# Second mixture of experts: the second product with the activations stationary and w2 streaming, 16 of 144 tokens on four column tiles

## Chip, cores, metric

One core of a Trainium2 chip runs the whole program. The metric is the device time of one execution in microseconds (us). PE is TensorE (matmul), PEld its loading of stationary operands, DVE VectorE, ACT ScalarE, POOL GpSimd, SP SyncE.

## What is computed

```python
attn_out = _attn_ref(q, k, v)                       # 2 x 8 heads x 576 x 64, with rotary positions
x = attn_out.transpose(0, 2, 1, 3).reshape(1152, 512)
x = _moe_ref(x, w_gate, w1, w2)                     # every expert for every token, weighted
return _moe2_ref(x, w_gate, w1, w2)                 # one expert for each token

def _moe2_ref(x, w_gate, w1, w2):
    N, D = x.shape; E = w_gate.shape[1]; cap = N // E      # 1152, 512, 8, 144
    logits = x @ w_gate
    ...                                             # greedy: best pairs first, at most cap tokens an expert
    for e in range(E):
        mask = assigned == e
        out[mask] = np.maximum(x[mask] @ w1[e], 0.0) @ w2[e]     # w1[e] 512x1024, w2[e] 1024x512
```

All data are float32. The change touches only the loop at the end, the second mixture: eight experts of exactly 144 tokens each.

## The kernel before

The attention takes the first 150 us or so, the first mixture lasts until about 945 us, and the second mixture (`moe2`, from L167) ends the program. Its tokens lie in a DRAM buffer `ysc`, row by row.

The assignment runs in phases (`phase(p)`). A phase finds, on DVE and PE, one expert that is full and its 144 tokens: `bcast` (L206) transposes the tokens' best logits, `compare` (L225) and `count` (L235, L241) count how many are better, `assign`, `total` and `close` find the full expert, `left` (L278) adds the phase's tokens to `ac` on POOL, `select` (L284) takes this expert's tokens, `place` (L300) and `spread` (L308) give each a slot and a one-hot row `hot`, and `index` (L316) multiplies `hot` with the token numbers: two groups of nine matmuls, 72 slots each. `address` makes row numbers of them, `gather` (L331) fetches the rows from `ysc` with two indirect DMAs on POOL into `xa` and `xb`, 72 tokens each, and `weights` (L344) issues eight DMAs of 512 KB on SP for w1 and w2 of this expert.

An expert (`expert(p)`, L404) then does four things on PE, all in plain float32:
- `tin` (L407): in two halves, transposes `xa` and `xb` (L413, L414), so that features lie on partitions: `xg`, 128 x 4 x 144. ACT copies them out of PSUM (L415).
- `h_mm` (L417, L422): 8 x 4 calls, stationary a 128x128 block of w1, moving 144 tokens; ACT applies the Relu into `h`, 128 x 8 x 144 (L425).
- `y_mm` (L427, L432): 4 x 8 calls, stationary a 128x128 block of w2, moving the 144 tokens of `h`; the result has features on partitions, and ACT copies it into `y` (L435).
- `tout` (L437, L441): two times four transposes bring tokens back onto partitions; ACT copies (L442), and `scatter` (L444) writes 72 rows a time to `out` with indirect DMAs on POOL (L447).

What stands where is set by a small planner (`Plan`, L121). Each step is added with the steps that it waits for and with its estimated durations per engine, as ("PE", 0.246, 0.0); the products (`main=True`) form a line whose order is fixed, and all other steps are emitted when the estimate says that they can start, before a product if they are earlier. The whole step is emitted at once, its ACT part with its PE part, so this order is also that of ACT's, DVE's and POOL's queues. A mark ("tn", p) keeps the input transposes of an expert from being placed earlier than `LEAD` products before its first one. PSUM tiles come from a ring of four banks (`ybank`).

Of the kernel before, what the change touches and what calls it, by code (L numbers as in the profile page):

```python
# [21 lines left out]
F32 = mybir.dt.float32  # L22
# [10 lines left out]
CAP = N // E  # L33
HC = CAP // 2
NT = N // 128
# [61 lines left out]

def moe2_consts(nc, one, rt):
# [12 lines left out]
    nc.gpsimd.tensor_copy(c["meta"].rearrange("p t k -> p (t k)"), rc[:, 288:324])  # L111
    for n, shape, dt, val in (("ones_b", [128, 128], BF, 1.0), ("pen", [128, E], F32, 0.0), ("u", [128, NT], F32, 1.0),
                              ("rem", [128, E], F32, float(CAP)), ("ac", [128, NT, E], F32, 0.0)):
        c[n] = one.tile(shape, dt, name=n)
        nc.gpsimd.memset(c[n], val)
    c["spacer"] = one.tile([1, 1], F32, name="spacer")
    c["tick"] = one.tile([1, 1], I32, name="tick")
    return c
# [44 lines left out]

CFG = dict(CG=3, NCMP=6, HA=20, LEAD=8, FILL=24)


def moe2(tc, nc, ctx, ps, m1, w1b, w2b, ident, lg, ysc, out):  # L167
    BIG = 3.0e38
    FAR = 1.0e6
    if True:  # L170
# [19 lines left out]
        def phase(p):  # L190
# [125 lines left out]
            def index():  # L316
                pi = ps.tile([128, 512], F32, name="PV", bufs=1)[0:HC, 0:8]
                for h in range(2):
                    for t in range(NT):
                        nc.tensor.matmul(pi[:, 4 * h:4 * h + 4], d["hot"][:, t, h * HC:(h + 1) * HC], meta[:, t],  # L320
                                         start=(t == 0), stop=(t == NT - 1))
                d["pi"] = pi

            def address():
                f = two.tile([HC, 8], F32, name="idf")
                V.tensor_copy(f, d["pi"])
                ix = two.tile([HC, 4], I32, name="ix", bufs=8)
                V.scalar_tensor_tensor(ix, f[:, 0:8:2], 128.0, f[:, 1:8:2], op0=OP.mult, op1=OP.add)
                d["ix"] = ix

            def gather():  # L331
                if "p" not in X:
                    m1.mst.close()
                    X["p"] = ctx.enter_context(tc.tile_pool(name="m2x", bufs=2))
                xa = X["p"].tile([HC, D], F32, name="xa")
                xb = X["p"].tile([HC, D], F32, name="xb")
                for h, x in enumerate((xa, xb)):
                    G.indirect_dma_start(out=x, out_offset=None, in_=ysc,
                                         in_offset=bass.IndirectOffsetOnAxis(ap=d["ix"][:, 2 * h:2 * h + 1], axis=0))
                d["xa"], d["xb"] = xa, xb  # L340
                if p == 0:
                    G.memset(tick, 0)

            def weights(lo, hi):  # L344
# [59 lines left out]
        def expert(p):  # L404
            d = S_[p]

            def tin(h):  # L407
# [3 lines left out]
                for k in range(2):  # L411
                    o = slice((2 * h + k) * 128, (2 * h + k + 1) * 128)
                    nc.tensor.transpose(pt[:, k, 0:HC], d["xa"][:, o], ident[0:HC, 0:HC])  # L413
                    nc.tensor.transpose(pt[:, k, HC:CAP], d["xb"][:, o], ident[0:HC, 0:HC])  # L414
                nc.scalar.activation(Z["xg", p][:, 2 * h:2 * h + 2], pt, AF.Copy)  # L415

            def h_mm(f, kt):  # L417
                if f == 0 and kt == 0:
                    Z["h", p] = X["p"].tile([128, FB, CAP], F32, name="h")
                if f % 2 == 0 and kt == 0:  # L420
# [3 lines left out]
                if f % 2 and kt == KT - 1:  # L424
                    nc.scalar.activation(Z["h", p][:, f - 1:f + 1], Z["ph"], AF.Relu)  # L425

            def y_mm(b, f):  # L427
                if b == 0 and f == 0:
                    Z["y", p] = X["p"].tile([128, KT, CAP], F32, name="y")
                if b % 2 == 0 and f == 0:  # L430
                    Z["py"] = m1.ybank()[:, 0:2 * CAP].rearrange("p (k c) -> p k c", k=2)
                nc.tensor.matmul(Z["py"][:, b % 2], d["wb"][f // 4][:, f % 4, b * 128:(b + 1) * 128],  # L432
                                 Z["h", p][:, f], start=(f == 0), stop=(f == FB - 1))
                if b % 2 and f == FB - 1:
                    nc.scalar.activation(Z["y", p][:, b - 1:b + 1], Z["py"], AF.Copy)  # L435

            def tout(h):  # L437
                o = Z["o", p, h] = X["p"].tile([HC, D], F32, name="o" + "ab"[h])
                pt = m1.ybank()
                for k in range(KT):  # L440
                    nc.tensor.transpose(pt[0:HC, k * 128:(k + 1) * 128], Z["y", p][:, k, h * HC:(h + 1) * HC], ident)  # L441
                nc.scalar.activation(o, pt[0:HC], AF.Copy)  # L442

            def scatter():  # L444
                for h in range(2):
                    G.memset(spacer, 0.0)
                    s = G.indirect_dma_start(  # L447
                        out=out, out_offset=bass.IndirectOffsetOnAxis(ap=d["ix"][:, 2 * h + 1:2 * h + 2], axis=0),
                        in_=Z["o", p, h], in_offset=None)
                    for q in scat:  # L450
                        tc.declare_no_dep(s.ins, q.ins, reason="each token has one expert")
                    scat.append(s)

# [10 lines left out]
            for b in range(4):  # L464
                for f in range(FB):
                    end = f == FB - 1 and b % 2
                    seg = [("PE", 0.246, 0.2), ("ACT", 0.29, 0.15)] if end else [("PE", 0.246, 0.0)]
                    op("yend" if end and b == 3 else ("y", b, f), ["whi", f"h{f | 1}"], seg, y_mm, b, f, main=True)
            for h in range(2):
                op(f"to{h}", ["yend"] + (["to0"] if h else []), [("PE", 0.5, 0.2), ("ACT", 0.6, 0.1)], tout, h)  # L470
            op("sc", ["to1"], [("POOL", 2.1, 0.0)], scatter)

# [21 lines left out]
        for p in range(1, E):  # L494
            plan.mark(("tn", p), nf + 2 * FB * KT * p - CFG["LEAD"])
        plan.run()
# [6 lines left out]
class Moe1:  # L503
# [37 lines left out]
    def open2(self):  # L541
# [4 lines left out]
        c2 = st.enter_context(tc.tile_pool(name="m2c", bufs=1))  # L546
        self.c2 = moe2_consts(nc, c2, self.rt)
        self.mst = ExitStack()
# [995 lines left out]
```

## Time and profile before

| | |
|---|---|
| time, median of 3 runs | 1132.48 us (1130.39 to 1133.1) |
| the profiled execution's own time | 1128.46 us |
| its span from first to last instruction | 1126.5 us |
| mean granted clock of PE | 0.998 |
| PE busy | 1101.4 us, 98% |
| DVE, ACT, POOL busy | 761.1, 367.6, 451.2 us |

The page gives the busy time of each engine, then the span in 40 slices of 28 us, then the chain of work that ended last. The second mixture's products fill the last six slices. Idle time of an engine costs only where another, which sets the end, waits for it. Matmuls overlap in the engine, so the duration of one is longer than its distance to the next; distances are read from the timeline.

### The profile page before, as it was taken

How to read it: one execution, taken by the hardware profiler on the slowest of the kernel's cores; microseconds unless marked ns; L12 is line 12 of the kernel's file. 1: busy time of each engine (PE TensorE's matmuls, PEld its weight loads, DVE VectorE, ACT ScalarE, POOL GpSimd, SP SyncE). 2: the span in 40 equal slices, each digit the busy share in tenths (PEclk: the TensorE clock that was granted, in tenths of full speed). 3: DMA queues.
4: the chain of work that ended last, by engine and by line, in shares of the span. 5: the costliest groups of instructions: out<-in, count | busy, mean ns of one | idle time of the engine just before them, and what ended most of it. 6: DMA issues, size and time to landing. Idle time of an engine off the chain costs nothing. (4 is left out here: it accounts for less than half of the span.)

```text
span 1126.5 us, 20911 instructions
## 1 busy us (share of the span) xinstructions
PE 1101.4 (98%) x8171; PEld 959.3 (85%) x8171; DVE 761.1 (68%) x1713; ACT 367.6 (33%) x846; POOL 451.2 (40%) x446
## 2 busy tenths in 40 slices
PE   6999999999999999999999999999999999999997
PEld 3666678998888889898888898998989876999997
DVE  5777733574677778777777776666679887988100
ACT  5777742143223232232232322333231111222222
POOL 6878452065434345444354443444210001554211
PEclk9999999999999999999999999999999999999999
DMA  5332322002222323332223321121140004978820
GB/s 130 79 74 50 98 81 76 1 1 71 83 87 88 94 76 105 112 94 83 87 87 126 97 70 62 39 75 38 38 150 29 1 29 141 351 242 289 278 76 22
DMA packets 105314, 107.22 MB, mean 95 GB/s; under 512 B 35456, under 2 KB 68608, under 8 KB 105088
## 3 DMA queue, kind: packets, MB, share of 16 engines
q1 hardware_dynamic: 102528, 100.66, 28.5%
q0 software_dynamic: 2048, 4.72, 1.3%
q8 instruction: 64, 1.05, 0.4%
q10 hardware_dynamic: 640, 0.51, 0.2%
q14 instruction: 34, 0.28, 0.1%
HBM read 98.85 MB, written 4.72 MB: 92 GB/s over the span
## 5 line engine op out<-in xcount | busy, mean ns | idle before, releaser
L929 DVE SCALAR_TENSOR_TENSOR acc<-Y,pw,acc 128x512 f32<-128x512 f32 x216 | 158.2, 742 | 1.5 <-PE Y L927 0.4
L865 PE MATMUL T<-xH,wa 128*128 128x256 f32 (+1 forms) x576 | 137.5, 294 | 0.2 <-ACT v L885 0.2
L865 PEld LDWEIGHTS T<-big,wb 128*128 128x128 f32 x864 | 125.7, 188 | 10.5 <-DVE v L878 1.4
L878 DVE TENSOR_TENSOR v<-T,v 128x256 f32<-128x256 f32 (+1 forms) x240 | 108.3, 451 | 38.6 <-PE T L865 35.8
L865 PE MATMUL T<-big,wb 128*128 128x256 f32 (+1 forms) x864 | 132.7, 296 | 0.0
L865 PEld LDWEIGHTS T<-xH,wa 128*128 128x128 f32 x576 | 100.0, 188 | 7.8 <-ACT v L885 1.9
L682 PE MATMUL T<-xH,wa 128*128 128x384 f32 x336 | 92.9, 337 | 0.0
L774 POOL TENSOR_TENSOR wa<-wraw,wa 128x512 fp32r<-128x512 f32 (+1 forms) x48 | 48.9, 1019 | 103.6 <-ACT wa L773 103.6
L865 PE MATMUL T<-xL,wa 128*128 128x256 f32 (+1 forms) x288 | 84.5, 293 | 0.0
L872 DVE SCALAR_TENSOR_TENSOR hlB<-v,hhB 128x320 fp32r<-128x320 f32 x72 | 57.0, 791 | 38.7 <-ACT hhB L871 38.7
L871 ACT ACTIVATE hhB<-v 128x320 fp32r<-128x320 f32 x72 | 34.0, 472 | 136.2 <-DVE v L878 136.2
L871 ACT ACTIVATE hhA<-v 128x256 fp32r<-128x256 f32 x72 | 30.1, 418 | 146.8 <-DVE v L878 146.8
L927 PE MATMUL Y<-wb,hhB 128*128 128x512 f32 x240 | 75.3, 396 | 0.0
L927 PE MATMUL Y<-wa,hhB 128*128 128x512 f32 x240 | 75.3, 395 | 0.0
L872 DVE SCALAR_TENSOR_TENSOR hlA<-v,hhA 128x256 fp32r<-128x256 f32 x72 | 50.5, 702 | 35.3 <-ACT hhA L871 35.3
L1000 DVE SCALAR_TENSOR_TENSOR fr<-fr,fc 128x512 f32<-128x512 f32 x64 | 52.5, 820 | 31.0 <-DMA fr<-in_moe_w 31.0
L793 POOL TENSOR_TENSOR wb<-wraw,wb 128x512 fp32r<-128x512 f32 x24 | 30.6, 1298 | 102.2 <-ACT wb L792 102.2
L793 POOL TENSOR_TENSOR wa<-wraw,wa 128x512 fp32r<-128x512 f32 x24 | 30.6, 1295 | 100.0 <-ACT wa L792 100.0
L701 PE MATMUL Y<-wb,hh 128*128 128x512 f32 x216 | 68.3, 397 | 0.0
L682 PEld LDWEIGHTS T<-xH,wa 128*128 128x128 f32 x336 | 61.3, 188 | 2.9 <-issue 0.9
L1352 DVE TENSOR_REDUCE negmax<-S 128x1 f32<-128x576 f32 x72 | 53.9, 749 | 14.4 <-PE S L1343 13.4
L927 PE MATMUL Y<-wa,hhA 128*128 128x512 f32 x192 | 60.0, 393 | 0.0
(323 smaller groups left out, 2668.3 us busy)
## 6 DMA issues: line engine op xcount, KB each, us to landing
wraw<-in_moe_w SPq DMA_DIRECT2D x52, 512.0 KB, 5.2
fr<-in_moe_w SPq DMA_DIRECT2D x64, 256.0 KB, 4.4
wraw<-in_moe_w SPq DMA_DIRECT2D x48, 256.0 KB, 3.2
big<-in_moe_w SPq DMA_DIRECT2D x20, 512.0 KB, 7.4
wa<-in_moe_w SPq DMA_DIRECT2D x18, 512.0 KB, 5.5
wb<-in_moe_w SPq DMA_DIRECT2D x14, 512.0 KB, 7.6
fc<-in_moe_w_gate SPq DMA_DIRECT2D x9, 256.0 KB, 3.5
ysc<-acc SPq DMA_DIRECT2D x9, 256.0 KB, 2.1
```

The lines of the kernel that those rows point to most:

```text
L682: nc.tensor.matmul(p[:, :CH], w[:, wi, kt, (fb % 2) * 128:(fb % 2) * 128 + 128], x[:, kt, o], start=(n == 0), stop=(n == 11))
L701: nc.tensor.matmul(self.Y[c][t], a[:, o], w[:, wi, fb % 2], start=(fb == 0 and n == 0), stop=(fb == FB - 1 and n == 2))
L774: G.tensor_tensor(l, src, h.bitcast(F32), op=OP.subtract)
L793: G.tensor_tensor(d["W"][:, 1, h], r[:, 2 + h], d["W"][:, 0, h].bitcast(F32), op=OP.subtract)
L865: nc.tensor.matmul(bank[:, 0:n], d[t][:, ww, b, r * 128:(r + 1) * 128], x(xw, r), start=(first and i == 0), stop=(i == 5), skip_group_chec ...
L871: A.activation(HH[:, f, o], src, AF.Relu)
L872: V.scalar_tensor_tensor(HL[:, f, o], src, 0.0, HH[:, f, o].bitcast(F32), op0=OP.max, op1=OP.subtract)
L878: V.tensor_tensor(o, bank[:, 0:n], x, op=OP.add)
L927: nc.tensor.matmul(y, h[:, f, o], w[:, ww, f], start=(f == 0 and z == 0), stop=(f == 1 and z == 2))
L929: V.scalar_tensor_tensor(self.acc[:, t], y, self.pw[:, t, e:e + 1], self.acc[:, t], op0=OP.mult, op1=OP.add)
L1000: nc.vector.scalar_tensor_tensor(r, r, 1.0, self.fc, op0=OP.mult, op1=OP.mult, accum_out=self.wf[:, f, e:e + 1])
L1352: V.tensor_reduce(m[0:n], SS[P, i][0:n, :, :288], axis=AX.XY, op=OP.max, negate=True)
```

## The change

The second product is turned round. For 128 of an expert's 144 tokens `h` is now the stationary operand (128 features x 128 tokens) and a row block of w2 moves, 512 columns: 8 calls in place of 32, and the result has tokens on partitions, so the output transposes go. The other 16 tokens (`RM`) are done by `y_rm`: eight calls with 32 stationary columns (16 tokens and 16 zero columns, for which `h` is padded to 160), dealt out over four column tiles of the array by their PSUM partitions 0, 32, 64 and 96, two calls each. ACT copies the four partial sums into `r`, and `add` sums them with a matmul by a constant 0/1 matrix `pick` (128x16), built at the start on POOL. The gathers and scatters are of 128 and 16 rows, so the input transposes are of 128 and of 16 tokens. `LEAD` is 4, and the planner gets new estimates: 0.46 us for a call of `y_mm`, 1.0 for `y_rm`, 0.5 for `add`.

```diff
-HC = CAP // 2
+RM = 16
+MN = CAP - RM
...
+    c["pick"] = one.tile([128, RM], F32, name="pick")
+    nc.gpsimd.tensor_tensor(c["pick"], ident[:, 0:RM], ident[:, 32:32 + RM], op=OP.add)
+    for i in (64, 96):
+        nc.gpsimd.tensor_tensor(c["pick"], c["pick"], ident[:, i:i + RM], op=OP.add)
...
-CFG = dict(CG=3, NCMP=6, HA=20, LEAD=8, FILL=24)
+CFG = dict(CG=3, NCMP=6, HA=20, LEAD=4, FILL=24)
...
-                        nc.tensor.matmul(pi[:, 4 * h:4 * h + 4], d["hot"][:, t, h * HC:(h + 1) * HC], meta[:, t],
+                        nc.tensor.matmul(pi[:, 4 * h:4 * h + 4], d["hot"][:, t, (RM, 0)[h]:(CAP, MN)[h]], meta[:, t],
...
+                    X["h"] = [X["p"].tile([128, FB, CAP + RM], F32, name=f"h{i}", bufs=1) for i in range(2)]
+                xa = X["p"].tile([MN, D], F32, name="xa")
+                xb = X["p"].tile([RM, D], F32, name="xb")
...
                 if p == 0:
                     G.memset(tick, 0)
+                    for t in X["h"]:
+                        G.memset(t[:, :, CAP:], 0.0)
...
-                    nc.tensor.transpose(pt[:, k, 0:HC], d["xa"][:, o], ident[0:HC, 0:HC])
-                    nc.tensor.transpose(pt[:, k, HC:CAP], d["xb"][:, o], ident[0:HC, 0:HC])
+                    nc.tensor.transpose(pt[:, k, 0:MN], d["xa"][:, o], ident)
+                    nc.tensor.transpose(pt[:, k, MN:CAP], d["xb"][:, o], ident[0:RM, 0:RM])
...
+            def y_mm(f):
+                if f == 0:
+                    Z["py"] = m1.ybank()
+                nc.tensor.matmul(Z["py"], Z["h", p][:, f, 0:MN], d["wb"][f // 4][:, f % 4], start=(f == 0),
+                                 stop=(f == FB - 1))
+
+            def y_rm():
+                Z["pr"] = m1.ybank()
+                for f in range(FB):
+                    o = f % 4 * 32
+                    nc.tensor.matmul(Z["pr"][o:o + 32], Z["h", p][:, f, MN:MN + 32], d["wb"][f // 4][:, f % 4],
+                                     start=(f < 4), stop=(f >= 4))
+                Z["r", p] = X["p"].tile([128, D], F32, name="r")
+                nc.scalar.activation(Z["r", p], Z["pr"], AF.Copy)
+
+            def add():
+                nc.tensor.matmul(Z["pr"][0:RM], c2["pick"], Z["r", p], start=True, stop=True)
+                o = Z["o", p, 1] = X["p"].tile([RM, D], F32, name="ob")
+                nc.scalar.activation(o, Z["pr"][0:RM], AF.Copy)
+
+            def tout():
+                o = Z["o", p, 0] = X["p"].tile([MN, D], F32, name="oa")
+                nc.scalar.activation(o, Z["py"], AF.Copy)
...
+            for f in range(FB + 1):
+                at = 6 if p == E - 1 else FB
+                if f == at:
+                    op("rm", ["whi", f"h{FB - 1}"], [("PE", 1.0, 0.2), ("ACT", 0.6, 0.1)], y_rm, main=True)
+                if f < FB:
+                    end = f == FB - 1
+                    op("yend" if end else ("y", f), ["whi", f"h{f | 1}"], [("PE", 0.46, 0.2 if end else 0.0)], y_mm, f,
+                       main=True)
+            op("to", ["yend"], [("ACT", 0.6, 0.1)], tout)
+            op("add", ["rm"], [("PE", 0.5, 0.2), ("ACT", 0.6, 0.1)], add)
             for h in range(2):
-                op(f"to{h}", ["yend"] + (["to0"] if h else []), [("PE", 0.5, 0.2), ("ACT", 0.6, 0.1)], tout, h)
-            op("sc", ["to1"], [("POOL", 2.1, 0.0)], scatter)
+                op(f"sc{h}", [("to", "add")[h]], [("POOL", 1.1, 0.0)], scatter, h)
...
-            plan.mark(("tn", p), nf + 2 * FB * KT * p - CFG["LEAD"])
+            plan.mark(("tn", p), nf + (FB * KT + FB + 1) * p - CFG["LEAD"])
```

In the changed file L422 and L423 are the input transposes, L431 is the first product, L439 the second (128 tokens), L446 the 16 tokens, L452 the sum over the tiles, L458 the copy of the 128 rows, L462 the scatter.

Three places show how the planner's order changes. The first is PE at the border from expert 6 to expert 7. Before:

```order
L432 MATMUL Y<-h,wa 128x144
L413 MATMUL Y<-ident,xa 128x72
L414 MATMUL Y<-ident,xb 128x72
L413 MATMUL Y<-ident,xa 128x72
L414 MATMUL Y<-ident,xb 128x72
L432 MATMUL Y<-h,big_11964 128x144 x4
L422 MATMUL Y<-xg,big_12106 128x144 x2
L422 MATMUL Y<-xg,wraw 128x144
L441 MATMUL Y<-ident,y 72x128 x4
```

The same border with the change:

```order
L439 MATMUL Y<-big_11966,h_10114 128x512 x2
L422 MATMUL Y<-ident,xa 128x128
L423 MATMUL Y<-ident,xb 128x16
L422 MATMUL Y<-ident,xa 128x128
L423 MATMUL Y<-ident,xb 128x16
L446 MATMUL Y<-wa,h_10114 32x512 x4
L446 MATMUL Y<-big_11966,h_10114 32x512 x4
L452 MATMUL Y<-r,pick 16x512
L431 MATMUL Y<-xg,big_12101 128x144 x2
```

The output transposes between the next expert's first products are gone; the 16 tokens' calls stand between the input transposes and the next expert, and here the sum L452 follows them at once (one border earlier four calls of L431 stand between).

The second place is the end of ACT's queue, the copies of the last expert. Before:

```order
L425 ACTIVATE h<-Y 128x288 x4
L435 ACTIVATE y<-Y 128x288 x2
L442 ACTIVATE oa<-Y 72x512
L442 ACTIVATE ob<-Y 72x512
L1540 UNCONDITIONAL_BRANCH
```

With the change:

```order
L434 ACTIVATE h_10115<-Y 128x2x144 x4
L449 ACTIVATE r<-Y 128x512
L454 ACTIVATE ob<-Y 16x512
L458 ACTIVATE oa<-Y 128x512
L1559 UNCONDITIONAL_BRANCH
```

The copy of the 16 rows now stands ahead of that of the 128 rows, and POOL's last two scatters stand in the same order.

The third place is POOL's queue in the middle of the assignment, around the second scatter of a row pair. Before:

```order
L338 DMA xa<-ysc,ix 72x512
L338 DMA xb<-ysc,ix 72x512
L446 MEMSET spacer 1x1
L447 DMA out<-oa,ix 1152x512
L446 MEMSET spacer 1x1
L447 DMA out<-ob,ix 1152x512
L280 TENSOR_TENSOR ac<-ac,a 128x72
```

With the change:

```order
L344 DMA xa<-ysc,ix 128x512
L344 DMA xb<-ysc,ix 16x512
L285 TENSOR_TENSOR ac<-ac,a 128x72
L461 MEMSET spacer 1x1
L462 DMA out<-oa,ix 1152x512
L461 MEMSET spacer 1x1
L462 DMA out<-ob,ix 1152x512
```

The first expert's scatters no longer stand between a gather and the sum into `ac`, but behind both.

## Rows read from the trace of the kernel before

**Rows 1.** The page: busy times; slices (PE, PEclk, GB/s); chain by engine and line.

```profile
PE 1101.4 (98%) x8171; PEld 959.3 (85%) x8171; DVE 761.1 (68%) x1713; ACT 367.6 (33%) x846; POOL 451.2 (40%) x446
...
PE   6999999999999999999999999999999999999997
...
PEclk9999999999999999999999999999999999999999
...
GB/s 130 79 74 50 98 81 76 1 1 71 83 87 88 94 76 105 112 94 83 87 87 126 97 70 62 39 75 38 38 150 29 1 29 141 351 242 289 278 76 22
...
PE 9%; issue 1%; DVE 1%; POOL 0%; ACT 0%; POOLq 0%; ACTq 0%
PE Y L432 4%; PE Y L422 4%; PE T L241 1%; PE Y L441 0%; POOL out L447 0%; PE T L209 0%; DVE hot L313 0%; PE PV L320 0%; PE Y L413 0%; PE Y L414 0%; DVE sel L295 0%; DVE seltmp L294 0%; DVE selb L297 0%; PE PV L304 0%; DVE tot L263 0%
```

**Rows 2.** Two stretches, one expert each: busy us (instructions) by engine, clock, DMA.

```profile
core 0: us, PE busy (x) PEld busy (x) DVE busy (x) ACT busy (x) POOL busy (x), PEclk, DMA share, GB/s
1066.30:1083.50 17.20, 17.20 (x148) 17.18 (x146) 0.00 (x0) 4.36 (x10) 4.12 (x7) 1.00 0.51 160
1083.50:1100.70 17.20, 17.20 (x148) 17.18 (x146) 0.00 (x0) 4.37 (x10) 2.04 (x4) 1.00 0.06 18
```

**Rows 3.** Timeline of PE in an expert: start us, length us, engine, line, stationary, moving, count.

```profile
1076.07 6.29 PE L432 MATMUL Y<-h,big 128*128 128x144 f32 x50
1082.20 0.23 PE L413 MATMUL Y<-ident,xa 72*128 72x72 f32 x1
...
1082.45 0.95 PE L432 MATMUL Y<-h,big 128*128 128x144 f32 x6
...
1085.26 0.60 PE L441 MATMUL Y<-ident,y 128*72 128x128 f32 x4
```

**Rows 4.** Instructions of L422, its four matmul rows (duration ns min/median/max).

```profile
L422 PE MATMUL Y<-xg,wa x192: 286/286/369, 956.7 to 1093.1; 128*128 128x144 f32 x192
...
L422 PE MATMUL Y<-xg,wb x128: 286/286/369, 1003.3 to 1076.0; 128*128 128x144 f32 x128
...
L422 PE MATMUL Y<-xg,big x96: 286/286/369, 978.6 to 1109.8; 128*128 128x144 f32 x96
...
L422 PE MATMUL Y<-xg,wraw x96: 286/286/369, 980.2 to 1110.3; 128*128 128x144 f32 x96
```

**Rows 5.** Timeline of PE while it waits for the first gather.

```profile
946.75 0.82 PE L241 MATMUL T<-oh,cmp 128*128 128x8 bf16 x27
947.43 3.18 PE L484 MATMUL Y<-hot,ones_b 128*128 128x512 bf16 x14
```

**Rows 6.** Timeline of PE in the attention, around a product on two column tiles.

```profile
59.81 0.35 PE L1310 MATMUL T<-ident,big 64*128 64x64 f32 x6
60.09 1.68 PE L1382 MATMUL PV<-pt,big 128*64 128x288 f32 x12
61.70 0.76 PE L1343 MATMUL S<-qk 64*128 64x288 f32 x4
```

**Rows 7.** Timeline of PE around the gating's transposes of 16 partitions.

```profile
177.66 0.34 PE L682 MATMUL T<-xL,wa 128*128 128x384 f32 x1
177.83 0.34 PE L682 MATMUL T<-xH,wa 128*128 128x384 f32 x1
178.10 0.73 PE L623 MATMUL PV<-ident,acc 16*128 16x16 f32 x9
178.76 0.73 PE L701 MATMUL Y<-wb,hh 128*128 128x512 f32 x2
179.33 0.39 PE L701 MATMUL Y<-wb,hl 128*128 128x512 f32 x1
```

**Rows 8.** Timeline of PE at an index product.

```profile
1011.19 0.79 PE L320 MATMUL PV<-meta,hot 128*72 128x4 bf16 x18
```

**Rows 9.** Timeline, all engines, around the longest wait of PE in the assignment.

```profile
988.99 0.94 POOL L447 DMA_INDIRECT out<-ob,ix  x1 [0.21 <-issue]
...
990.32 0.23 DVE L294 TENSOR_TENSOR seltmp<-ac,new 128x72 f32<-128x72 f32 x1 [1.83 <-POOL ac L280]
...
991.09 0.18 PE L302 MATMUL PV<-selb,bef_b 128*128 128x9 bf16 x1 [1.54 <-DVE selb L297]
```

**Rows 10.** Timelines of PE, ACT and POOL at the end; POOL at the first gather.

```profile
1117.27 1.14 PE L432 MATMUL Y<-h,wb 128*128 128x144 f32 x8
...
1119.41 0.59 ACT L442 ACTIVATE oa<-Y 72x512 f32<-72x512 f32 x1 [0.55 <-PE Y L441]
...
1121.54 0.93 POOL L447 DMA_INDIRECT out<-ob,ix  x1 [0.22 <-issue]
...
950.45 1.15 POOL L338 DMA_INDIRECT xa<-ysc,ix  x1 [17.76 <-DVE cmp L232]
```

More of the change, by code (lines that the diff above doesn't have):

```diff
@@ L95, with moe2_consts @@
 TINY = 2.0 ** -120
-def moe2_consts(nc, one, rt):
+def moe2_consts(nc, one, rt, ident):
     c = {}
@@ L316, in index @@
             def index():
-                pi = ps.tile([128, 512], F32, name="PV", bufs=1)[0:HC, 0:8]
+                pi = ps.tile([128, 512], F32, name="PV", bufs=1)[:, 0:8]
                 for h in range(2):
                     for t in range(NT):
-                        nc.tensor.matmul(pi[:, 4 * h:4 * h + 4], d["hot"][:, t, h * HC:(h + 1) * HC], meta[:, t],
+                        nc.tensor.matmul(pi[:, 4 * h:4 * h + 4], d["hot"][:, t, (RM, 0)[h]:(CAP, MN)[h]], meta[:, t],
                                          start=(t == 0), stop=(t == NT - 1))
@@ L324, in address @@
             def address():
-                f = two.tile([HC, 8], F32, name="idf")
+                f = two.tile([128, 8], F32, name="idf")
                 V.tensor_copy(f, d["pi"])
-                ix = two.tile([HC, 4], I32, name="ix", bufs=8)
+                ix = two.tile([128, 4], I32, name="ix", bufs=8)
                 V.scalar_tensor_tensor(ix, f[:, 0:8:2], 128.0, f[:, 1:8:2], op0=OP.mult, op1=OP.add)
@@ L334, in gather @@
                     X["p"] = ctx.enter_context(tc.tile_pool(name="m2x", bufs=2))
-                xa = X["p"].tile([HC, D], F32, name="xa")
-                xb = X["p"].tile([HC, D], F32, name="xb")
+                    X["h"] = [X["p"].tile([128, FB, CAP + RM], F32, name=f"h{i}", bufs=1) for i in range(2)]
+                xa = X["p"].tile([MN, D], F32, name="xa")
+                xb = X["p"].tile([RM, D], F32, name="xb")
                 for h, x in enumerate((xa, xb)):
                     G.indirect_dma_start(out=x, out_offset=None, in_=ysc,
-                                         in_offset=bass.IndirectOffsetOnAxis(ap=d["ix"][:, 2 * h:2 * h + 1], axis=0))
+                                         in_offset=bass.IndirectOffsetOnAxis(ap=d["ix"][0:(MN, RM)[h], 2 * h:2 * h + 1],
+                                                                                axis=0))
                 d["xa"], d["xb"] = xa, xb
@@ L418, in h_mm @@
                 if f == 0 and kt == 0:
-                    Z["h", p] = X["p"].tile([128, FB, CAP], F32, name="h")
+                    Z["h", p] = X["h"][p % 2]
                 if f % 2 == 0 and kt == 0:
@@ L424, in h_mm @@
                 if f % 2 and kt == KT - 1:
[L425 to L452, printed above, removed]
+                    nc.scalar.activation(Z["h", p][:, f - 1:f + 1, 0:CAP], Z["ph"], AF.Relu)
@@ new lines, in add, with scatter @@
+            def add():
[5 more added lines that the diff above has]
+                nc.scalar.activation(o, Z["py"], AF.Copy)
+            def scatter(h):
+                G.memset(spacer, 0.0)
+                s = G.indirect_dma_start(
+                    out=out, out_offset=bass.IndirectOffsetOnAxis(ap=d["ix"][0:(MN, RM)[h], 2 * h + 1:2 * h + 2], axis=0),
+                    in_=Z["o", p, h], in_offset=None)
+                for q in scat:
+                    tc.declare_no_dep(s.ins, q.ins, reason="each token has one expert")
+                scat.append(s)
@@ L463, in expert @@
                     op(f"h{f}" if kt == KT - 1 else ("h", f, kt), ["wlo", f"tin{kt // 2}"], seg, h_mm, f, kt, main=True)
[L464 to L468, printed above, removed]
+            for f in range(FB + 1):
[8 more added lines that the diff above has]
+            op("add", ["rm"], [("PE", 0.5, 0.2), ("ACT", 0.6, 0.1)], add)
             for h in range(2):
-                op(f"to{h}", ["yend"] + (["to0"] if h else []), [("PE", 0.5, 0.2), ("ACT", 0.6, 0.1)], tout, h)
-            op("sc", ["to1"], [("POOL", 2.1, 0.0)], scatter)
+                op(f"sc{h}", [("to", "add")[h]], [("POOL", 1.1, 0.0)], scatter, h)
         for n, (f, save) in enumerate(m1.tail()):
@@ L546, in open2 @@
         c2 = st.enter_context(tc.tile_pool(name="m2c", bufs=1))
-        self.c2 = moe2_consts(nc, c2, self.rt)
+        self.c2 = moe2_consts(nc, c2, self.rt, self.ident)
         self.mst = ExitStack()
```

## The prediction, made before the change was run

> **What bounds the kernel now.** Start with the page: TensorE (PE) is busy in 98% of the span at full clock [rows 1]. Since a busy PE need not be a PE at its limit, look next at the chain that ended last: its two largest lines are PE's, L432 and L422, the two products of the second mixture, and PE has 9% of the span in that chain against 1% for any other engine [rows 1]. Then the stretches: in 1066.3 to 1083.5 us and again in 1083.5 to 1100.7 us PE is busy for all of 17.20 us, while VectorE has nothing to do, ScalarE 4.4 us and GpSimd 2 to 4 us [rows 2]. One such stretch is one expert. The timeline of one shows what fills it [rows 3]: eight input transposes, 64 passes of the first product, 64 of the second, eight output transposes, back to back. So each pass that PE gains or loses here moves the end. Elsewhere the order of PE stays as it was, so I count PE's passes in this stage, expert by expert.
>
> **The price of a pass.** A timeline group lasts to the end of its last matmul, so its pitch is (length less one duration) by (count less one). For 144 columns: (6.29 - 0.29)/49 = 0.122 us; for 128: (0.60 - 0.27)/3 = 0.11; for 72: 0.0625 [rows 3]. Each f32 product is two passes: 512 records of L422, in four rows, for 8 x 32 calls [rows 4]. From 72 to 144 columns a pass costs 0.85 ns per column, whatever the width of the weights. For 512 columns no f32 row exists. The nearest is the bf16 fill: (3.18 - 0.38)/13 = 0.215 us for 512 columns [rows 5], 0.42 ns a column, half of what the f32 rows pay. Twice that is 0.43 us, and 512 x 0.85 ns is 0.435. I take 0.43; the lower bound is the bf16 row itself, 0.215 (about 0.23 with its overhead), which is also what the planner's new figure of 0.46 us for two passes assumes.
>
> The Trainium skill, "TensorE: Matmul & The Clock Gate", section "Back-to-back issue gap", gives a stream of weight loads and matmuls 81 ns a matmul at 128 columns and 131 ns at 512; with an f32 pass taken as two of these the second product would cost 16 x 0.262 = 4.2 us, and the change would gain. The trace disagrees: 0.215 us at 512 columns, with weights loaded before each [rows 5].
>
> **The change, part by part, for one expert.**
> Second product, 128 tokens: 64 passes x 0.122 = 7.83 us become 8 calls x 2 passes x 0.43 = 6.88. **-0.95.**
>
> The 16 remaining tokens: 8 calls, 16 passes of 512 columns on four column tiles. That column tiles run side by side is in the attention's L1382, two tiles of 64: its 12 passes of 288 columns start within 1.68 - 0.41 = 1.27 us, five steps of 0.25 [rows 6], where one after the other would need eleven. I take four at a time: 4 x 0.43 = 1.72 us. The bound above is two at a time, 3.44.
>
> A change of the tile shape costs as well. Nine transposes of 16 partitions stand between full-size passes in the gating of the first mixture [rows 7]. L682 keeps 0.17 us; after its last start at 177.83 the next comes at 178.10: 0.10 too late. L623's last start is 178.10 + 0.73 - 0.21 = 178.62, the next 178.76: 0.14 where its pitch is 0.065. The pass after that starts 0.34 later (0.73 - 0.39), where 0.23 is usual: 0.11 more. L1382 shows the same: L1343 starts 0.34 after its last start, where 0.24 is due, and on the way in 0.15 where 0.06 is due, its first step being 0.05 longer (1.27 for five steps of 0.243) [rows 6]. So going in costs 0.10 + 0.05 and coming back 0.10 + 0.11: 0.36 for the group. L446: 1.72 + 0.36 = **+2.08.** Stationary operands of 72 rows or 72 columns show no such gap [rows 3], so today's stage pays none; that is the lower bound, zero.
>
> Input transposes: now 128 and 16 tokens in turn, twice per half. The 16-token ones are of the form of L623, so each half is full, narrow, full, narrow, full. With these gaps [rows 7] and a 0.11 pitch: 0.21 into the first narrow one, 0.14 out, 0.26 (0.11 + 0.05 + 0.10) in again, 0.14 out, 0.11 on the next product's second pass: 0.85 a half, 1.70 against 8 x 0.0625 = 0.50. **+1.20.** (Without the switches 4 x 0.11 + 4 x 0.065 = 0.70.)
>
> The sum over the four tiles (pick): 2 x 0.43 + 0.33 = 1.19, against eight output transposes, 8 x 0.11 = 0.88, which go. **+0.31**, in seven experts; the eighth has both in the tail.
>
> Index product: its weights grow from 72 to 128 columns. 72 take (0.79 - 0.17)/17 = 0.036 us, L241's 128 take (0.82 - 0.17)/26 = 0.025 [rows 5, 8]: 18 x 0.011 = -0.2, in seven experts **-1.3** (the first lies beside the wait for the saves).
>
> Stalls: at 989.5 PE waits 1.54 us for L297, behind it DVE 1.83 us for `ac` on GpSimd, which stands behind a scatter of 0.94 us [rows 9]. In the new order `ac` comes before the scatters: **-1.5.** In expert 6 `add` stands right behind `rm` and has to wait for ScalarE's copy of 128x512, 0.17 + 0.59 us [rows 10], less the switch that it spares: **+0.6.** Elsewhere at least 0.9 us of PE work lies between. The planner counts y passes at half my price; real PE work between the steps of the assignment is therefore longer than planned, and VectorE comes early, not late.
>
> Beside other work: gathers and scatters of 128 and 16 rows (0.93 to 1.15 us for 72 [rows 9, 10]; same 144 rows in sum) and the two new memsets, on a GpSimd that is idle for over 10 us of each 17 [rows 2]; the ScalarE copies (ScalarE has 12 us free). Weight loads keep their order on SP; each expert's index now comes about one expert ahead, some 20 us, for transfers of 8 x 512 KB, 12 us at the 351 GB/s of the fastest slice [rows 1].
>
> Tail: from the start of the last y pass, 1118.12, to the last scatter's issue, 1121.54, are 3.42 us today [rows 10]. Afterwards: `add` 0.53 + 0.05 + 0.43 + 0.59 = 1.60, ScalarE copies `ob`, then `oa`, which stands behind it, to 2.85, GpSimd scatters `ob` from 2.35 to 3.3 and `oa` from 3.6. That is +0.2, less 0.3 for where the last pass is counted, plus 0 to 0.7 if 128 rows take longer than 72: **+0.2.**
>
> Sum: 8 x (2.08 + 1.20 - 0.95) = 18.6; 7 x 0.31 = 2.2; -1.3; -1.5; +0.6; +0.2: **+18.8 us** on the profiled 1128.46 us, 1147.3. That execution lies 4.0 us below the median of 1132.48; on the median it is **1151 us**. About 0.3% (3.4 us) is what a measurement of this kernel can tell from no change.
>
> **Rivals.**
> A, fewer tiles at once. The attention shows two [rows 6]; four moving streams were not seen. Two at a time: 8 x 1.72 = 13.8 more, 1165. One at a time: 8 x 5.2 = 41 more, 1193. The Trainium skill, same page, section "Part 3: Packing small matmuls", says matmuls start strictly in order; a call's second pass would then hold back the next tile's first, nine steps instead of four, 1168. The attention is against it [rows 6]: six calls that way need six steps between first and last start, and there are five.
>
> B, cheap switches. If the gaps at the borders [rows 6, 7] were operand waits (both groups begin a new operand), the price falls from 8 x (1.00 + 0.36) + 7 x 0.33 = 13.2 to nothing: 1138. Against: 0.10 appears at each of four such borders.
>
> C, faster. A long stream costs one cycle per column in f32 too, as in bf16: 0.23 us a pass. Then y is 3.68 (-4.15), `rm` 0.92 + 0.36, `add` 0.79: 8 x (-4.15 + 1.28 + 1.20) - 0.6 - 2.0 = -16, so 1116. It decides below 0.32 us a pass: the sum is 174 passes (8 x 20 + 7 x 2) times the price, less 56. For it is only the plan's figure; against it, 288 columns in the attention cost 0.243 [rows 6], twice the bf16 rate.
>
> **How the numbers follow.** My sum 0.75; A 0.12 (0.09 for two at a time); B 0.08; C 0.05. The range runs from B's 1138 to the upper end of A with two tiles, 1168; outside are C, one tile at a time, and mixtures. C is the chance of faster, 0.05; within 0.3% lies only B with a longer idle time recovered, 0.03; slower 0.92.
>
> **What would show it.** In the profile after: L439 at a pitch near 0.43 us and 0.59 long; L446 in four starts together, 16 passes within some 1.4 us of first to last start; a start of L423 0.2 us after L422's and 0.14 before the next; a stretch of an expert without assignment work of 19.5 to 20 us instead of 17.20. Wrong if L439's pitch is near 0.23, if L446 takes 3.5 us or more, if L422 and L423 alternate without gaps, or if PE has waits of a microsecond for weights or for VectorE.

## The result and the profile after

The changed kernel takes 1144.84 us (median of 4, 1141.47 to 1145.46) against 1131.43 us (1128.25 to 1133.1) for the kernel before: ratio 1.0116 [1.0084, 1.0147], 13.4 us slower. A second measurement (e0_same) gave 1145.76 against 1131.84, ratio 1.0119 [1.0103, 1.0134]. The forecast was 1151.0 us, 18.8 more than before, in a range from 1138 to 1168: direction and range held, the size was 0.71 of the forecast. The profiled executions differ by more, 1143.4 against 1126.5 us of span; what the profiles say of that is told below.

The page of the changed kernel, busy times and granted clock, to be held against [rows 1]:

```profile
PE 1123.8 (98%) x7867; PEld 924.7 (81%) x7867; DVE 762.6 (67%) x1713; ACT 365.1 (32%) x838; POOL 439.4 (38%) x451
...
PEclk8999999999999999999999999999999998999999
```

PE is busy for 22.4 us more with 304 matmuls fewer. Two slices, the first and the 34th (about 944 to 972 us), have a clock below 0.9, where [rows 1] have none.

One expert without assignment work, from the start of one remainder to the next (columns as in [rows 2]):

```profile
1095.29:1114.79 19.50, 19.50 (x108) 12.39 (x107) 0.00 (x0) 4.14 (x9) 2.07 (x4) 1.00 0.36 132
```

Again PE is busy from end to end at full clock, for 19.50 us where [rows 2] have 17.20. The timeline of PE shows of what (columns as in [rows 3]):

```profile
1095.29 1.92 PE L446 MATMUL Y<-big,h 128*32 128x512 f32 x16
1097.15 1.25 PE L431 MATMUL Y<-xg,wa 128*128 128x144 f32 x8
1098.32 1.03 PE L452 MATMUL Y<-r,pick 128*16 128x512 f32 x2
1099.29 0.88 PE L431 MATMUL Y<-xg,wa 128*128 128x144 f32 x5
...
1106.25 3.60 PE L439 MATMUL Y<-wa,h 128*128 128x512 f32 x8
1109.68 1.88 PE L439 MATMUL Y<-big,h 128*128 128x512 f32 x4
1111.40 0.27 PE L422 MATMUL Y<-ident,xa 128*128 128x128 f32 x1
1111.60 0.23 PE L423 MATMUL Y<-ident,xb 16*128 16x16 f32 x1
1111.76 0.33 PE L422 MATMUL Y<-ident,xa 128*128 128x128 f32 x1
1112.02 0.23 PE L423 MATMUL Y<-ident,xb 16*128 16x16 f32 x1
1112.18 1.98 PE L439 MATMUL Y<-big,h 128*128 128x512 f32 x4
...
1114.00 0.27 PE L422 MATMUL Y<-ident,xa 128*128 128x128 f32 x1
1114.21 0.23 PE L423 MATMUL Y<-ident,xb 16*128 16x16 f32 x1
1114.37 0.33 PE L422 MATMUL Y<-ident,xa 128*128 128x128 f32 x1
1114.62 0.23 PE L423 MATMUL Y<-ident,xb 16*128 16x16 f32 x1
1114.79 1.06 PE L446 MATMUL Y<-wa,h 128*32 128x512 f32 x8
```

Four readings. **L439**: eight passes in 3.43 us from 1106.25 to the next group, 0.43 us a pass. **L446**: 16 passes of 512 columns last 1.86 us to the next start; one after the other they would need 16 x 0.43 = 6.9, so four tiles run side by side. **Input transposes**: 0.20, 0.16, 0.26, 0.16 us between starts, 0.78 for a half, and the group of four L439 behind it is 1.98 us long where its like is 1.88. **The sum, L452**: 0.97 us, and each neighbour pays for the border: eight L431 take 1.17 us to the next start (8 x 0.122 = 0.98), the five behind it 0.88, (0.88 - 0.29)/4 = 0.147 a pass where 0.122 is usual.

The rows of the weight loads (PEld) show something of what a border is:

```profile
1110.97 0.14 PEld L422 LDWEIGHTS Y<-ident,xa 128*128 128x128 f32 x1 [0.24 <-issue]
...
1111.60 0.13 PEld L423 LDWEIGHTS Y<-ident,xb 16*128 16x128 f32 x1 [0.49 <-issue]
1111.76 0.14 PEld L422 LDWEIGHTS Y<-ident,xa 128*128 128x128 f32 x1
```

Behind a product of the same shape the load for L422 starts 0.43 us ahead of its pass (1111.40). On either side of the narrow transpose the load starts only with its own pass, at 1111.60 and 1111.76. That the load which isn't done ahead is the whole price of a border is not shown.

The second product of the last expert but one shows the one wait that was foreseen; column 6 has the idle time and its releaser:

```profile
1117.49 1.03 PE L452 MATMUL Y<-r,pick 128*16 128x512 f32 x2 [0.78 <-ACT r L449]
```

What was not foreseen is the clock. PE, DVE and the other columns are those of [rows 2]; the stretches lie at the first expert:

```profile
954.00:956.00 2.00, 1.57 (x7) 0.64 (x7) 1.76 (x13) 0.07 (x1) 0.32 (x1) 1.00 0.53 66
956.00:958.00 2.00, 1.84 (x15) 1.32 (x16) 1.83 (x5) 0.59 (x2) 0.00 (x0) 0.52 0.86 322
958.00:960.00 2.00, 2.00 (x11) 2.00 (x10) 1.38 (x6) 1.28 (x4) 0.00 (x0) 0.50 1.05 398
960.00:962.00 2.00, 2.00 (x26) 1.91 (x25) 1.58 (x6) 0.35 (x1) 0.06 (x1) 0.50 1.04 382
962.00:964.00 2.00, 2.00 (x14) 2.00 (x14) 2.00 (x6) 0.27 (x1) 1.70 (x2) 0.78 1.04 383
```

For some 6 us PE stands at 0.50, the 1.2 GHz level, right after it had waited at 953 us (0.93 us for VectorE) and in the gaps of the first input transposes. In the kernel before these stretches are at 1.00, though it waits longer there (0.75, 1.09 and 0.26 us); one of them:

```profile
956.00:958.00 2.00, 1.74 (x28) 1.53 (x27) 1.92 (x4) 1.56 (x4) 0.00 (x0) 1.00 1.05 403
```

### The profile page after: what moved, and what is told of

It is laid out like the page before. It is cut to its first block, busy times and chain, and to the rows that moved or that the text cites. A ratio compares the mean times of both kernels' runs of the same rounds, so it can differ in the third digit from the quotient of the medians.

```text
span 1143.4 us, 20331 instructions
## 1 busy us (share of the span) xinstructions
PE 1123.8 (98%) x7867; PEld 924.7 (81%) x7867; DVE 762.6 (67%) x1713; ACT 365.1 (32%) x838; POOL 439.4 (38%) x451
## 4 chain that ended last, share of the span: by engine, by line
PE 94%; issue 3%; DVE 1%; POOL 1%; DMA 0%; ACT 0%; SPq 0%; POOLq 0%; DVEq 0%; ACTq 0%
PE Y L946 26%; PE T L884 23%; PE Y L720 9%; PE T L701 9%; PE Y L431 4%; PE Y L439 4%; PE T L1401 3%; PE S L1362 3%; PE T L1329 3%; PE T L246 1%; PE Y L446 1%; PE PV L1329 1%; PE T L214 1%; PE PV L1401 1%; PE S L1366 0%
## 5 line engine op out<-in xcount | busy, mean ns | idle before, releaser
L946 PE MATMUL Y<-wb,hhA 128*128 128x512 f32 x192 | 60.0, 393 | 0.0
```

Source lines behind the costliest of these rows:

```text
L946: nc.tensor.matmul(y, h[:, f, o], w[:, ww, f], start=(f == 0 and z == 0), stop=(f == 1 and z == 2))
```

## The experiments

Times in this section are medians; ratios are to the kernel before on the same chip.

**e0_same**, the changed kernel again.

> The changed kernel again, unchanged, for the size of the loss and for the granted clock. In its first profile the clock stood at 1.2 GHz from about 956 to 963 us, after PE had waited in 952.6 to 954 us and 955.5 to 956.2 us for the first gather, and from about 11 to 21 us in the attention. Theory one (the loss is the count of PE passes and of tile-shape borders, 2.3 us an expert): 12 to 15 us over the kernel before, whether or not the clock falls at 956 us; a fall adds some 3 us. Rival (the fall of the clock at the first gather comes with the change and is a fixed part of its loss): the fall is there again at the same place, in this run and in every variant that keeps the input transposes.

1145.76 us, 1.0119 [1.0103, 1.0134]. That is 13.9 us over the kernel before, as theory one has it. Its profile has the clock's fall too, at 960 to 968 us; but the rival falls with e2 and e3, which keep the input transposes and have no fall there.

**e1_flat_in**, the 16-row tile padded to 128 partitions, so that all input transposes have one shape.

```diff
-nc.tensor.transpose(pt[:, k, MN:CAP], d["xb"][:, o], ident[0:RM, 0:RM])
+nc.tensor.transpose(pt[:, k, MN:256], d["xb"][:, o], ident)
```

> Only the input transposes change: the 16 gathered rows lie in a tile of 128 partitions whose other rows stay zero, and are transposed as a full 128x128 block, so that no narrow tile shape stands between full ones. Theory one (borders of the tile shape cost 0.1 to 0.2 us each): a half of the transposes takes 0.44 us in place of 0.78, the next product's first pass is not slowed by 0.10, only the border into the 16 tokens' product stays: 0.7 us an expert, 5.5 us in all (4.5 to 6.5) less than the changed kernel. Rival (the gaps are waits for operands and stay): the four wide passes more cost 0.1 us an expert, so nothing to 1 us slower.

1139.45 us, 1.0062 [1.0049, 1.0076]: 6.3 us less than e0, within what theory one expected. The transposes of one half (here L425 and L426), and the product behind them:

```profile
1106.37 0.27 PE L425 MATMUL Y<-ident,xa 128*128 128x128 f32 x1
1106.48 0.27 PE L426 MATMUL Y<-ident,xb 128*128 128x128 f32 x1
1106.59 0.27 PE L425 MATMUL Y<-ident,xa 128*128 128x128 f32 x1
1106.70 0.27 PE L426 MATMUL Y<-ident,xb 128*128 128x128 f32 x1
1106.81 1.88 PE L442 MATMUL Y<-big,h 128*128 128x512 f32 x4
```

Four steps of 0.11 us, 0.44 where 0.78 were, and the group behind is 1.88 us long, not 1.98. A transpose with eight times the columns is quicker than one that changes the tile's shape: 0.11 against 0.16 and the 0.09 that it adds before it. The weight load for the pass at 1106.48 starts at 1106.37, one pass ahead. So the borders, rival B's point, are real and most of the input's price.

**e2_wide_pick**, the sum's weights padded from 16 to 128 columns.

```diff
-nc.tensor.matmul(Z["pr"][0:RM], c2["pick"], Z["r", p], start=True, stop=True)
+nc.tensor.matmul(Z["pr"], wide, Z["r", p], start=True, stop=True)
```

> Only the sum over the tiles changes: pick is padded with zero columns to 128, so that this product has the full tile shape; its 112 further result rows are not used. Theory one: the two borders of L452 go, about 0.2 us an expert, 1.5 us in all (1 to 2.5), visible in the trace as the next full-size pass following at 0.43 us and the next at 0.12. Rival (the gaps around it are the wait for ScalarE's copy r): no change, the gaps stay.

1142.87 us, 1.0102 [1.0087, 1.0117], 2.9 us less than e0, more than the 1 to 2.5 expected. The borders do what was said:

```profile
1094.08 1.25 PE L434 MATMUL Y<-xg,wa 128*128 128x144 f32 x8
1095.16 1.02 PE L455 MATMUL Y<-r,wide 128*128 128x512 f32 x2
1096.02 1.76 PE L434 MATMUL Y<-xg,wa 128*128 128x144 f32 x13
```

1.08, 0.86 and 0.122 a pass, where the changed kernel has 1.17, 0.97 and 0.147: 0.09 + 0.11 + 0.10 = 0.30 us at this sum. It is the largest of seven: at the others the same comparison gives 0.11 (where PE waits for the sum anyway) to 0.25, 1.5 us in all, which is what was expected. The profile of this run has no fall of the clock at 956 us (1.00 from 954 to 964 us), which may be the rest; that is not shown.

**e3_no_rest**, without remainder, sum and scatter of the 16 rows (these rows are not written).

> Leaves out the 16 remaining tokens of each expert after the first product: no four-tile product, no sum over tiles, no scatter of 16 rows; the rest as in the changed kernel. Theory one: the four-tile product costs 1.96 us an expert with its borders, the sum 1.16 and one wait of 0.94, and the tail ends 2.3 us earlier: 15.7 + 8.1 + 0.9 + 2.3 = 27 us less than the changed kernel (24 to 29), so some 10 to 13 us faster than the kernel before. Rival (the planner's own prices, 1.0 and 0.5 us): 12 us less than the changed kernel, about as the kernel before.

1117.66 us, 0.9869 [0.9854, 0.9885], 28.1 us less than e0, within what was expected. So the turned product for 128 tokens would win 14 us over the kernel before if the last 16 tokens were free; they cost 28 (second product, sum and scatter; their input transposes are still in).

**e4_rest_w2_stationary**, e1 with the 16 tokens as the kernel before had them, w2 stationary.

```diff
-nc.tensor.matmul(Z["pr"][o:o + 32], Z["h", p][:, f, MN:MN + 32], d["wb"][f // 4][:, f % 4],
+nc.tensor.matmul(Z["pr"][:, b * RM:(b + 1) * RM], d["wb"][f // 4][:, f % 4, b * 128:(b + 1) * 128],
+                 Z["h", p][:, f, MN:CAP], start=(f == 0), stop=(f == FB - 1))
```

> The changed kernel with the 16 rows padded to 128 at the input (as in e1) and the remainder done without column tiles: w2 blocks stationary (64 passes of 16 columns), then four 128-column transposes in the place of the sum over tiles. Theory (the remainder's price is passes plus borders of the tile shape): L446 1.86 + 0.11 us becomes 64 passes of 0.026 us (what a pass of 128 weight columns and few moving columns takes in L246) = 1.6 us without a border, add about 1.0 becomes 4 x 0.11 = 0.44; so 0.9 us less an expert, 7 us less than e1: 1132.5 us (1130 to 1136). Rival (an f32 pass with 16 columns is not cheaper than one with 72, 0.0625): 4.0 us for the 64 passes, 1.5 us an expert more than e1: about 1151 us.

1211.89 us, 1.0716 [1.0697, 1.0736]: 72 us more than e1, and both expectations fall. PE in the last remainder but one:

```profile
1165.02 1.04 PE L451 MATMUL Y<-h,big 128*128 128x16 f32 x8
1165.91 1.04 PE L451 MATMUL Y<-h,wa 128*128 128x16 f32 x8
...
1169.30 1.87 PE L451 MATMUL Y<-h,big 128*128 128x16 f32 x8
1171.01 1.87 PE L451 MATMUL Y<-h,wa 128*128 128x16 f32 x8
```

At first eight passes take 0.89 us, 0.111 each, as long as a pass of 128 columns, though each has 16: a product's f32 pass with 128 columns of weights has a floor. From 1168 us on eight take 1.71 us, 0.214 each:

```profile
1168.00:1172.00 4.00, 4.00 (x20) 4.00 (x20) 0.00 (x0) 0.00 (x0) 0.00 (x0) 0.50 0.00 0
```

The clock fell to 0.50 while PE was issuing without a gap, but passes of few columns only. The floor is worth 64 x 0.111 - 1.86 = 5.2 us an expert, 42 in eight. The rest goes with the falls, which come back at one remainder after the other: from 980 to 1200 us the mean granted clock is 0.83, so some 0.17 x 220 = 37 us are lost there, an estimate (the mean of the whole run is 0.962, e1's 0.994). The bound I had taken, 0.026 us, is a bf16 row's.

The Trainium skill, "TensorE: Matmul & The Clock Gate", section "LDWEIGHTS (loading the stationary operand)", gives a load of weights a time by its columns alone, columns / 1.2 in ns; worked out for 128 that is an estimate of 107 ns. The 0.111 us at full clock agree; the 0.214 us at the lower level do not, since the formula gives one time for both levels.

**e5_prices**, the planner's prices set to the measured ones.

> The changed kernel with the planner's prices set to what the trace shows (input transposes 0.83, y 0.86, remainder 1.9, sum 1.05 us). Theory (the loss is PE's own work, the order costs one wait of 0.94 us): 1 to 2 us below the changed kernel's 1145.8, so about 1144.5 (1143 to 1146.5). Rival (half prices lead the planner astray, and the order is what loses): 1141 or less.

1146.60 us, 1.0130 [1.0111, 1.0149]: no gain. The rival falls, and the theory's 1 to 2 us are not seen. The wait of `add` shrinks from 0.78 to 0.2 us, but the order now puts two experts' index products shortly ahead of a remainder, and a new fall of the clock follows, with L446 at half speed (eight passes 1.89 us long instead of 1.06):

```profile
1054.88 0.60 PE L325 MATMUL PV<-meta,hot 128*128 128x4 bf16 x18
1056.00 0.59 PE L325 MATMUL PV<-meta,hot 128*128 128x4 bf16 x18 [0.52 <-DVE idf L331]
1056.45 1.10 PE L439 MATMUL Y<-big,h 128*128 128x512 f32 x2
1057.49 1.89 PE L446 MATMUL Y<-wa,h 128*32 128x512 f32 x8
```

The stretch around it, columns as above:

```profile
1057.00:1060.00 3.00, 3.00 (x16) 0.59 (x16) 0.00 (x0) 0.00 (x0) 1.82 (x3) 0.60 0.86 312
```

Whether that fall ate a gain of a microsecond is not shown; the prices were not what the change lost most of its 13 to 14 us by.

**e6_fill32**, 32 fills (`FILL=24` becomes `FILL=32`).

> The changed kernel with 32 instead of 24 fill matmuls (8 x 0.215 = 1.7 us more) where PE waits for the first expert's rows. Theory (the idle time there lets the granted clock fall to 0.50 at the start of the second mixture): the stretch behind the fills is at clock 1.00 and the kernel takes 2 us less, 1143.8 (1142 to 1145.5). Rival (the fall does not hang on that idle time, or costs nothing): the fills only come on top, 1145.8 to 1147.5.

1145.36 us, 1.0117 [1.0098, 1.0136], 0.4 less than e0: inside the theory's range, near its upper end, and not to be told from no gain. The clock does as the theory says:

```profile
956.00:958.00 2.00, 1.98 (x17) 1.01 (x15) 1.76 (x14) 0.02 (x1) 0.03 (x1) 1.00 0.42 54
958.00:960.00 2.00, 2.00 (x22) 1.51 (x19) 1.89 (x4) 0.83 (x3) 0.00 (x0) 1.00 1.01 393
```

From the last six passes of the first mixture to the third expert's first product are 61.47 us here, 62.74 in the changed kernel's profile, 62.71 in e0's (the first fill itself has no record in some traces). Over all profiles the fall at 956 us or just after is in four of seven with the change and 24 fills (not in e2, e3 and e4), in none of four with 32 fills (e6, e8, e10, e11), and in none of three in the order of before. At about 3 us a fall (worked out below) four in seven make 1.7 us on the average, as much as eight fills cost; that would be why the time stands still, an estimate from few executions.

**e7_before_ac_dve**, the kernel before with one addition moved.

```diff
-G.tensor_tensor(ac, ac, d["a"], op=OP.add)
+V.tensor_tensor(ac, ac, d["a"], op=OP.add)
```

> The kernel before with the one addition to ac moved from GpSimd to VectorE, nothing else. Theory (the stall of 1.5 us at 989 us is ac behind a scatter): 1131.8 less 1.5 to 1.9, plus up to 0.4 for the 0.23 us that VectorE takes on top: about 1130.3 (1129.5 to 1131.5). Rival (something else is late next, weights or indices): 1131.8, no change.

1130.33 us, but over 12 runs from 1128.01 to 1137.64; ratio 0.9997 [0.9979, 1.0014], so the time tells nothing. The waits of PE from 966 to 1060 us do: before

```profile
PE PV L302 <- DVE selb L297: 1.8, 2, 1.5
```

and here (total, times, longest)

```profile
PE PV L302 <- DVE selb L297: 0.3, 1, 0.3
```

The 1.5 us stall was `ac` on GpSimd, as [rows 9] said. Two idle times without a releaser, 0.5 us in all, are new in e7's list. In the changed kernel the list is empty.

**e8_rest_by_columns**, e1 and e6, and each column tile takes a quarter of the output columns over all of h, so that no sum is needed.

```diff
-nc.tensor.matmul(Z["pr"][o:o + 32], Z["h", p][:, f, MN:MN + 32], d["wb"][f // 4][:, f % 4],
+nc.tensor.matmul(Z["pr"][32 * b:32 * b + 32, 0:128], Z["h", p][:, f, MN:MN + 32],
+                 d["wb"][f // 4][:, f % 4, b * 128:(b + 1) * 128],
...
+nc.scalar.dma_start(o[:, b * 128:(b + 1) * 128], Z["r", p][32 * b:32 * b + RM])
```

> The changed kernel with three edits: input padded as in e1, 32 fills as in e6, and the remainder's four column tiles each take one quarter of the output columns over all eight blocks of h (64 passes of 128 columns, 32 weight columns each), so that no sum over tiles is needed; four small transfers on ScalarE's queue bring the pieces together. Theory (four tiles run side by side, a step is as long as its moving columns): 16 steps of 0.11 = 1.76 us, as much as L446 now; the sum's 0.97 us goes in seven experts and its wait of 0.94 in one, the transfers lengthen the tail by about 1, the fills give 0.4: 7.1 us less than e1's 1139.45, 1132.3 us (1130 to 1135). Rival (a small f32 pass has a floor of 0.11 us whatever the width of its weights, as e4's passes of 16 columns had): 64 x 0.11 = 7.1 us for the remainder, 5.2 us an expert more: 1174 us or more.

1140.81 us, 1.0083 [1.0068, 1.0098]. Neither: PE does its 64 passes in the time expected (see e11), but now waits from 960 to 1110 us

```profile
PE T L249 <- DVE cmp L240: 4.1, 7, 0.7
PE Y L425 <- DMA xa<-ysc,ix: 2.3, 1, 2.3
```

and ScalarE's queue shows why: four issues hold it for 2.90 us, and `mb`, which VectorE needs, is copied behind them.

```profile
1025.91 2.90 ACTq L458 DMA_DIRECT2D ob<-r  x4
...
1028.91 1.25 ACT L220 ACTIVATE mb<-T 128x384 f32<-128x384 f32 x3 [2.55 <-DVE ix L336]
```

The releaser named, `ix`, was done at 1028.55; the copy starts 0.10 us after the last issue. Behind two of these waits the granted clock fell as well, to 0.57 on the mean of 1034 to 1038 us and of 1092 to 1096 us, which costs on top.

**e9_before_ac_index**, e7 with 128 columns of weights in 17 of 18 index passes.

> The kernel before with ac on VectorE (e7) and, in addition, an index product whose weights are 128 columns wide in 17 of 18 passes instead of 72 (the extra rows are not used). Theory (the prediction's term of 0.2 us an expert for the index): 1.2 us less than e7's 1130.3, so 1129.1 (1128 to 1130.5). Rival (index passes lie beside a wait in most experts): as e7, 1130.3.

1130.15 us (1127.36 to 1133.08), 0.9983 [0.9968, 0.9997]: the only complete version that comes out below the kernel before, by 0.2%, and the interval barely leaves out no change. Its difference to e7 can't be told in the time, but in the row of the index product, to be held against [rows 8]:

```profile
1048.87 0.60 PE L323 MATMUL PV<-meta,hot 128*128 128x4 bf16 x18 [0.41 <-DVE idf L329]
```

**e10_all_borders**, e1, e2 and e6 together.

> The changed kernel with the input padded (e1), the sum's weights padded to 128 columns (e2) and 32 fills (e6) together. Theory (borders of the tile shape and the fall of the clock are separate and add up): e1's 1139.45 less 0.2 an expert for the sum's borders (1.4) and 1 to 2 for the clock: 1136.6 us (1135 to 1138.3). Rival (e2's 2.9 us were the clock alone): 1138 to 1139.5.

1137.08 us, 1.0051 [1.0038, 1.0063]. The median lies in the theory's range, but the interval, 1136.2 to 1139.1 us on the kernel before in this measurement, reaches into the rival's 1138 to 1139.5: the two are not told apart.

**e11_rest_by_columns_sp**, e8 with the four transfers on SyncE (`nc.sync.dma_start`).

> As e8, but the four small transfers that bring the remainder's pieces together are issued by SyncE and not by ScalarE. Theory (e8 lost what it won because ScalarE's queue was held for 2.9 us by the four issues of each expert, so that mb came late, VectorE after it, and PE waited 4.1 us for cmp and 2.3 us for xa): those 6.4 us go, 1134.4 us (1132 to 1136.5). Rival (the waits come from the order that the planner makes without the sum, not from that queue): no gain, 1139 to 1142.

1134.77 us, 1.0042 [1.0028, 1.0056], 6.0 us less than e8 (4.6 by the two ratios, since e8 was measured on another chip) and within 0.4 of the theory. The waits for `cmp` and `xa` are gone, the copies of `mb` follow ScalarE's other work at once, and up to PE's last passes the profile has no fall of the clock, so the 6 us hold both e8's waits and its two falls. The remainder without a sum:

```profile
1103.27 1.08 PE L449 MATMUL Y<-wa,h 128*32 128x128 f32 x32
1104.17 1.06 PE L449 MATMUL Y<-big,h 128*32 128x128 f32 x32
1105.15 0.76 PE L434 MATMUL Y<-xg,big 128*128 128x144 f32 x4
```

1.88 us for 64 passes, where L446's 16 took 1.86. By its median it is the best form of the change (e10's interval overlaps), and still slower than the kernel before.

## Why the prediction was right, and where its size was off

**What bounds it.** Right: in both stretches PE has no idle time, and what e1, e2 and e3 took from PE there came off the end.

**Price of a pass.** Right: 0.43 us, not the bf16 row's 0.215. Rival C is out. The 131 ns that the Trainium skill, "TensorE: Matmul & The Clock Gate", section "Back-to-back issue gap", gives for 512 columns are met by neither row.

**Four tiles at once.** Right: 1.86 us with the way in counted in the transposes ahead, against 1.72 + 0.36. Rival A is out, also in the form that a call's second pass holds back the next tile's first: nine steps instead of four would have shown. The trace shows when passes start, not in which order they were issued, so it does not decide on the strict order of starts itself that the Trainium skill states (same page, section "Part 3: Packing small matmuls").

**Borders.** Right in kind, by two padded kernels, and for the input nearly in size: 6.3 us, where by the forecast's prices 8 x (1.70 - 8 x 0.11) = 6.6 goes. The sum's were taken too high: 0.33 each, 2.3 us for seven, measured 0.11 to 0.30, 1.5 us (e2). Rival B is out.

**The term that was off: one expert.** Forecast -0.95 + 2.08 + 1.20 + 0.31 = 2.64 us, measured 19.50 - 17.17 (from one expert's first product to the next one's, in the stretches of [rows 2]) = 2.33, so 0.31 less. The terms of the new stage add up to the 19.50: transposes 0.88 + 0.79, first product 7.83, y 6.88, remainder 1.86 + 0.09, sum 1.17. About half the excess is a border counted twice: the second half of the transposes ends directly in the remainder (1114.62 to 1114.79), so the way back to full size in the one and the way in to the other are the same border. The other half is in the stage before: its terms add up to 17.04, and it took 17.17.

In the experts beside the assignment it is more. From the first expert's first product to the eighth's PE is busy for 142.63 us before and for 156.37 us in e6, which has the order of the change and no fall of the clock there. Without the index products in these stretches (7 x 0.64 and 6 x 0.47 us from start to start) that is 15.4 us over seven experts, 2.20 each where 2.64 was forecast: some 3 us too much. The cheaper borders of the sum are 0.8 of it; the rest is not taken apart.

**Index.** Right: 18 passes in 0.60 us instead of 0.79, and e9 shows the same for the old order. The Trainium skill, same page, section "Weight-path perf modes — Fast Weight Load (FWL) and DoubleRow", says that weights of all 128 columns that are not f32 load faster; the trace agrees, (0.60 - 0.16)/17 = 0.026 us a pass for 128 columns, 0.036 for 72 [rows 8]. Seven products are busy for 4.25 us where they were for 5.44: -1.2, and -1.3 was taken.

**Stalls.** Named rightly, credited too low: -1.5 was taken for the one at 989 us. The changed kernel has no listed wait from 966 to 1060 us, the one before 2.1 us there (1.8 for L297 and 0.3 for an index); and at the first expert it waits 0.93 + 0.39 us where the kernel before waits 0.75 + 1.09 us for its two gathers and 0.26 us for an index. Expert 6's wait came as said, 0.78 us. From 952 us to the last expert's first product PE's listed waits go from 4.2 to 2.1 us in all: -2.1 where -1.5 + 0.6 was taken, 1.2 us more.

**Tail.** From the start of the last y pass at 1134.88 to the last scatter's issue at 1138.49 are 3.6 us, 0.2 more than [rows 10], as forecast.

**Not in the sum: the clock.** From the last six passes of the first mixture to the third expert's first product the changed kernel's profile needs 62.74 us and e2's 59.40, whose program differs there by two sums, 0.5 us: about 3 us is the price of the fall. The two profiles, one with it and one without, differ by 17 us, the medians by 13.4 to 13.9; that the fall makes this difference fits, but how many of the other executions have it is not shown. Another fall, at 12 to 20 us in the attention, is in the changed kernel's profile (0.50) and not in that of before, but it belongs to neither: with the same order there, e7 and e9, built on the kernel before, have it (0.64 and 0.61), e2, e8 and e11 have not. A third, at 914 to 924 us (0.83 on the mean), ahead of the second mixture, is in seven of the 14 profiles, e7's and e9's among them and not that of before. So the misses of the sum, some 3 us too much for the experts and 1.2 too little credit for the stalls, against nothing for the clock, partly cancelled, which was luck.

Open: why the fall at 956 us comes in some executions and not in others, and one idle time of 0.92 us in e2 at 1082 us that has no releaser in the trace.

## What to carry to other kernels

A product's f32 pass here costs the larger of its moving columns (0.85 ns each) and its weight columns' load (0.11 us for 128; a transpose's pass can be shorter, 0.0625 us with 72 columns moving [rows 3]), so turning a product round only pays where it saves more column-passes than the leftovers need; here 16 of 144 tokens cost 28 us, twice what the other 128 had won. Keep one tile shape on PE: padding with zeros to full size was quicker than a narrow instruction between wide ones, in both places where it was tried. When an edit takes work off PE, look at the queue to which it goes: the same four transfers cost 5 to 6 us more on ScalarE's queue than on SyncE's.

## What the runs showed of the hardware that was not expected

Four column tiles run at full rate side by side with 512 moving columns (16 passes in 1.86 us) and with 128 (64 in 1.88). A product's f32 pass of 16 columns with 128 columns of weights takes 0.111 us, as long as a pass of 128. The granted clock can fall to 0.50 without PE standing still: it did in e4 amid 64 passes of 16 columns. In e5 it fell behind 36 passes of 4 columns with 0.52 us of idle time between them. With eight fills more (1.7 us) it stayed at 1.00 in four profiles of four, in a wait where it fell in four of seven without them; so few profiles may be chance, and the fills were worth nothing that the time shows.
